# Newton steps and a scaling moved from VectorE and ScalarE to GpSimd, with a rewritten table of issue slots, in a fused attention and MLP kernel

## The chip, the core and the metric

One Trainium2 chip, one of its cores. The metric is the device time of one execution in microseconds (us), taken as the median of three runs. The five engines are TensorE (PE in the profile, with PEld for its weight loads), VectorE (DVE), ScalarE (ACT), GpSimd (POOL) and SyncE (SP, whose queue issues all DMAs here).

## What the program computes

```
def rmsnorm(x, g):
    rms = np.sqrt(np.mean(x * x, axis=-1, keepdims=True) + 1e-06)
    return x / rms * g
q_n, k_n = (rmsnorm(q, g_q), rmsnorm(k, g_k))
scores = (1.0 / np.sqrt(64)) * np.matmul(q_n, k_n.transpose(0, 1, 3, 2))
scores = scores - np.max(scores, axis=-1, keepdims=True)
attn = np.exp(scores)
attn = attn / (np.sum(attn, axis=-1, keepdims=True) + 1e-09)
attn_out = np.matmul(attn, v)                    # 8 batches, 12 heads, 448 tokens, 64 columns
x = attn_out.transpose(0, 2, 1, 3).reshape(3584, 768)
h = x @ w_in                                     # 768 x 2048
g = np.where(h > 0.0, h, np.exp(np.minimum(h, 0.0)) - 1.0)
out = g @ w_out                                  # 2048 x 768
```

All inputs and the output are float32.

## The kernel before

The matmuls run in float16. Each float32 operand is split into a high half and a low half (the rest after rounding), and a product is made of three matmuls: high by high, high by low, low by high.

The work is staged by batch. A batch has six pairs of heads (`p`, 48 in all) and each pair seven tiles of 128 queries (`T`, 336 in all). A tile passes: scores into one of five PSUM banks (`s_mm`, L547), row maximum on DVE (`s_max`, L559), exponential on ACT with its row sum (`s_exp`, L570), the sum plus 1e-9 on POOL (`s_z`, L577), the reciprocal on DVE (`s_rec`, L584), P's high half on ACT (`s_hi`, L609) and its low half on DVE (`s_lo`, L620), after which the bank is free for another tile. P is transposed by DMA (`s_tr`) or, for three pairs of the first batch, by PE with a diagonal that POOL makes (`s_diag`, `s_pe`). Seven tiles make an `attend(p)` on PE, whose output ACT and DVE evict (`x_high`, `x_low`).

Ahead of that, each pair's q and k are loaded, squared and summed; ACT makes a first inverse root from Ln and Exp (`qk_root`), and `qk_newton` (L384) sharpens it with one Newton step: four small DVE instructions on 128x14 numbers, at L387 (twice), L388 and L391. POOL multiplies by the result (`qk_norm`, L401).

The MLP of a batch starts when its six pairs are done. Each of its 16 hidden blocks ends in `m1_out` (L673): exp(h) on ACT (L682), `two`, (exp(h) - 1) times a scale on ACT (L686), a min and max against h on DVE (L690), then the high half on ACT (L695) and the low half on DVE (L698). The exponential's tile is called `e`.

While the first two batches run, the weights are converted too: `conv_in` for w_in's 16 blocks of 768 columns, `conv_out` for w_out's 24 of 512. Each takes two ACT instructions (L237, L238), two DVE instructions (L243, L267), a column sum on PE (L142), and steps on POOL (L291, or L322 and L331). Their working rooms are slices of three fixed tiles, `raws`, `wts` and `w32s`.

What sets the order of the work is a table, `SCHED`, written out by hand in half slots: two slots to a tile. A step listed at slot 14.5 is issued half a slot ahead of those at 15. Every engine executes its instructions in the order in which the slots issue them. A list `rate` says how many MLP matmuls have been issued by a given slot, so that they fill PE between the attention matmuls. From the third batch on one line of each kind is repeated.

Of the kernel before, what the change touches and what calls it, by code (L numbers as in the profile page):

```python
# [9 lines left out]
F16 = mybir.dt.float16  # L10
# [3 lines left out]
AF = mybir.ActivationFunctionType  # L14
ALU = mybir.AluOpType
# [8 lines left out]
NJ = 2 * S // 128  # L24
# [8 lines left out]
def tile_attention_then_elu_mlp(ctx: ExitStack, tc: tile.TileContext, qk, v, v_scan, gg, w_in, w_out, out):  # L33
# [184 lines left out]
    def conv(src, i, width, acol, bank, parts):  # L218
# [3 lines left out]
        raw = raw_in[i % len(raw_in)] if width == WI_W else room(raws, 2 * width, i)  # L222
        raw = raw.rearrange("p (n w) -> p n w", w=2)

        t, w = room(wts, width, i), room(w32s, width, i if width == WI_W else i + 2)
        ws = None

        def load():
# [154 lines left out]

    def qk_newton(p):  # L384
        ss, r0 = st1[p]
        for x, op0, op1 in ((D * 1e-6, ALU.add, ALU.mult), (-0.5 / D, ALU.mult, ALU.mult)):
            nc.vector.scalar_tensor_tensor(out=ss, in0=ss, scalar=x, in1=r0, op0=op0, op1=op1)  # L387
        nc.vector.scalar_tensor_tensor(  # L388
            out=r0, in0=ss, scalar=1.5, in1=r0, op0=ALU.add, op1=ALU.mult
        )  # L390
        nc.vector.tensor_scalar(  # L391
            out=r0[:, NJ:], in0=r0[:, NJ:], scalar1=kap, scalar2=None, op0=ALU.mult
        )
# [194 lines left out]

    def s_diag(T):
        dg = dgs[T] = pool.tile([128, 128], F32, tag="dgz", name="dgz", bufs=2)  # L590
        (nc.vector if DIAG_DVE else nc.gpsimd).tensor_scalar(
            out=dg, in0=ident, scalar1=stats[T][:, 2:3], scalar2=0.0, op0=ALU.mult, op1=ALU.add
        )

# [14 lines left out]
    def s_hi(T):  # L609
        if by_pe(T):  # L610
            ps, hi, _ = turned(T)
            nc.scalar.activation(hi, ps, AF.Copy)
            return
        if T < PB:
            p16 = p16s[T] = pfirst[(T - sum(p < T // NJ for p in PE_PAIRS) * NJ) % len(pfirst)]
        else:
            p16 = p16s[T] = pool.tile([128, 2 * S], F16, tag="p16", name="p16", bufs=3)
        nc.scalar.activation(p16[:, :S], pss[T][:, :S], AF.Copy, scale=stats[T][:, 2:3])  # L618
# [54 lines left out]
    def m1_out(b, f, ph):  # L673

        sc, isc, nisc, gsc = (t[:, f : f + 1] for t in mscale[b][:4])
        e = None
        g = gts[f]

        def one():
            nonlocal e  # L680
            e = pool.tile([128, S], F32, tag="e", name="e", bufs=3)
            nc.scalar.activation(e, ph[:, :S], AF.Exp, scale=sc)  # L682

        def two():

            nc.scalar.activation(e, e, AF.Identity, scale=isc, bias=nisc)  # L686

        def three():

            nc.vector.scalar_tensor_tensor(  # L690
                out=e, in0=e, scalar=0.0, in1=ph[:, :S], op0=ALU.min, op1=ALU.max
            )

        def four():
            nc.scalar.activation(g[:, 0], e, AF.Copy, scale=gsc)  # L695

        def five():
            nc.vector.scalar_tensor_tensor(  # L698
                out=g[:, 1], in0=e, scalar=gsc, in1=g[:, 0], op0=ALU.mult, op1=ALU.subtract
            )  # L700

        return [one, two, three, four, five]
# [84 lines left out]
    for T in reversed(range(NCHUNK)):  # L787
        k = 2 if by_pe(T) else 0 if T < PB else 1
        hs = [2 * T + h for h in SCHED["tile"][k]]
        j = T % NJ  # L790
        if k < 2:
            put(hs[:6], [(fn, T) for fn in (s_max, s_exp, s_z, s_rec, s_hi, s_lo)])


            at(hs[7 if j == 0 else 8 if j == NJ - 1 else 6], s_tr, T)
        else:
            put(hs, [(fn, T) for fn in (s_max, s_exp, s_z, s_rec, s_diag, s_pe, s_hi, s_lo)])
    for p in range(NP):
        k = p if p < 12 else 11
        put([h + HP * (p - k) for h in SCHED["qk"][k]], [  # L800
# [78 lines left out]
    for h in range(h + 1, h + 9):  # L879
# [3 lines left out]

SCHED = {
# [13 lines left out]
    ],  # L898
    "v": [
        [-2, 14, 15, 17, 18, 23, 24],  # L900
        [17, 23, 24, 24, 26, 36, 37],
        [26, 37, 38, 38, 40, 50, 51],
        [41, 52, 53, 54, 55, 65, 65],
        [54, 65, 66, 68, 68, 78, 79],
        [68, 79, 80, 82, 82, 93, 93],
        [82, 93, 94, 96, 96, 106, 106],
        [96, 107, 109, 109, 110, 120, 121],
        [110, 121, 122, 123, 124, 134, 135],
        [124, 135, 136, 137, 138, 147.5, 148.5],
        [138, 149, 150, 151, 152, 162, 162],  # L910
        [152.5, 163.5, 164.5, 165.5, 166.5, 176.5, 177.5],
    ],
    "scan": [
# [3 lines left out]
    ],  # L917
# [17 lines left out]
    ],  # L935
# [25 lines left out]
    ],  # L961
    "m": [
        [68, 69, 70, 72, 73, 74, 75, 77],
        [153, 154, 155, 156, 158, 159, 160.5, 161.5],
    ],
    "tile": [
# [3 lines left out]
    ],  # L970
    "rate": [
        [4, 8, 46, 104, 148, 188, 240, 288, 336, 382, 430, 478, 536, 576],
    ],
}
WO_OWN = 7

CK = S // 4
PE_PAIRS = (1, 3, 5)
DIAG_DVE = False

RATE_FROM = 85
UP = 13
# [38 lines left out]
```

## Time and profile before

| | us |
|---|---|
| median of 3 runs (lowest to highest) | 1270.25 (1269.4 to 1272.03) |
| the profiled execution, its own time | 1268.82 |
| its span | 1267.0 |
| PE busy | 1196.3 (94%) |
| DVE busy | 861.1 (68%) |
| ACT busy | 880.6 (70%) |
| POOL busy | 535.4 (42%) |

Busy time is the union of an engine's instructions in the trace. The difference between span and time is what lies around the program. Of the 40 equal slices of the span that the page shows, the first eight have a PE that is not fully busy; from the ninth slice on (from 260 us) it is busy throughout. The word head below means the first 260 us.

### The profile page before, as it was taken

To read this page: it belongs to the slowest core of one execution; us is meant where nothing else is said; L and a number is where in the kernel's file an instruction comes from. 1 tells how busy PE (TensorE), PEld (TensorE's weight loads), DVE (VectorE), ACT (ScalarE), POOL (GpSimd) and SP (SyncE) were. 2 spreads that over 40 slices of the span, in tenths; PEclk is the share of its full clock that TensorE was granted. 3 is DMA by queue.
4 is the path that set the end of the run, shared out by engine and by line. 5 is a ranking of instruction groups with operands and counts; after the bars stand their busy time and mean duration, and the time that the engine had idled before them with its cause. 6 is when DMAs were issued, how large, how long until landed. Compare 5 with 4: busy or idle time off the path is not lost.

```text
span 1267.0 us, 21793 instructions
## 1 busy us (share of the span) xinstructions
PE 1196.3 (94%) x7150; PEld 735.0 (58%) x7150; DVE 861.1 (68%) x1913; ACT 880.6 (70%) x1889; POOL 535.4 (42%) x858
## 2 busy tenths in 40 slices
PE   3778678999999999999999999999999999999998
PEld 2435444567556665576556755666557755676576
DVE  7888999986676567755785667756876677642310
ACT  6888789975797568855896578756886579643520
POOL 4766877664434343433434433334334333320000
PEclk9889799999999999999999999999999999999999
DMA  9967799999677986689577976798677968672012
GB/s 296 252 154 188 197 205 201 221 215 227 155 160 151 218 177 156 145 195 215 137 162 160 237 149 158 153 220 186 144 154 184 223 140 157 137 156 76 1 49 63
DMA packets 432979, 214.44 MB, mean 169 GB/s; under 512 B 389089, under 2 KB 409185, under 8 KB 432865
## 3 DMA queue, kind: packets, MB, share of 16 engines
q1 hardware_dynamic: 432864, 213.04, 74.1%
q8 instruction: 57, 0.93, 0.3%
q14 instruction: 58, 0.47, 0.1%
HBM read 93.52 MB, written 14.16 MB: 85 GB/s over the span
## 4 chain that ended last, share of the span: by engine, by line
PE 82%; DVE 10%; ACT 3%; POOL 3%; issue 1%; DMA 1%; SPq 0%; ACTq 0%; POOLq 0%
PE m L757 23%; PE m L743 20%; PE s L757 11%; PE s L743 10%; PE s L554 9%; PE av L658 7%; DVE w32s L267 2%; DVE st L561 1%; DVE wts L243 1%; DVE gall L698 1%; DVE p L628 1%; DVE ss L376 1%; DMA raws<-in_w_out 1%; PE s L599 1%; PE m L298 1%
## 5 line engine op out<-in xcount | busy, mean ns | idle before, releaser
L561 DVE TENSOR_REDUCE st<-s 128x1 f32<-128x448 f32 x336 | 208.3, 620 | 208.4 <-PE s L554 207.1
L579 POOL TENSOR_SCALAR st<-st 128x1 f32<-128x1 f32 x336 | 85.0, 253 | 496.7 <-ACT s L575 478.6
L743 PE MATMUL m<-x,whi 128*128 128x448 f16 x1020 | 281.9, 353 | 1.0 <-DVE x L669 1.0
L757 PE MATMUL m<-gall,whos 128*128 128x448 f16 x1024 | 282.2, 353 | 0.0
L757 PEld LDWEIGHTS <-whos 128*128 128x128 f16 x1536 | 221.5, 145 | 73.6 <-issue 1.1
L618 ACT ACTIVATE p<-s,st 128x448 f16<-128x448 f32 x294 | 185.9, 632 | 84.4 <-DMA pt<-p 51.1
L575 ACT ACTIVATE s<-s,st 128x448 f32<-128x448 f32 x315 | 190.5, 605 | 62.3 <-DVE st L561 62.1
L743 PEld LDWEIGHTS <-whi 128*128 128x128 f16 x1536 | 149.3, 98 | 136.1 <-issue 1.1
L628 DVE SCALAR_TENSOR_TENSOR p<-s,st,p 128x448 f16<-128x448 f32 x294 | 198.6, 676 | 14.0 <-ACT p L618 13.8
L554 PE MATMUL s<-qkt 128*128 128x448 f16 (+1 forms) x768 | 186.4, 363 | 19.6 <-DVE gall L625 11.2
L757 PE MATMUL m<-gall,wls 128*128 128x448 f16 x512 | 181.1, 354 | 0.0
L743 PE MATMUL m<-x,wli 128*128 128x448 f16 x510 | 179.8, 353 | 0.0
L743 PE MATMUL s<-x,whi 128*128 128x448 f16 x516 | 141.7, 352 | 0.0
L757 PE MATMUL s<-gall,whos 128*128 128x448 f16 x512 | 141.2, 353 | 0.0
L757 PEld LDWEIGHTS <-wls 128*128 128x128 f16 x768 | 110.6, 144 | 41.4 <-issue 6.5
L743 PEld LDWEIGHTS <-wli 128*128 128x128 f16 x768 | 75.1, 98 | 76.1 <-issue 8.4
L698 DVE SCALAR_TENSOR_TENSOR gall<-e,gsc,gall 128x448 f16<-128x448 f32 x128 | 98.5, 769 | 24.1 <-ACT gall L695 24.1
L554 PEld LDWEIGHTS <-qkt 128*128 128x128 f16 (+1 forms) x768 | 62.6, 101 | 86.0 <-issue 45.1
L658 PE MATMUL av<-pt,vt 128*64 128x448 f16 x990 | 102.0, 354 | 1.0 <-DVE most L145 1.0
L695 ACT ACTIVATE gall<-e,gsc 128x448 f16<-128x448 f32 x128 | 85.2, 666 | 18.1 <-DVE e L690 17.7
L686 ACT ACTIVATE e<-e,nisc,isc 128x448 f32<-128x448 f32 x128 | 97.1, 758 | 0.3
L665 ACT ACTIVATE x<-av 128x448 f16<-128x448 f32 x48 | 26.0, 542 | 96.1 <-PE av L658 70.1
(120 smaller groups left out, 1778.7 us busy)
## 6 DMA issues: line engine op xcount, KB each, us to landing
wls<-wl_d SPq DMA_DIRECT2D x48, 512.0 KB, 4.2
nat<-in_qk SPq DMA_DIRECT2D x48, 448.0 KB, 3.6
raws<-in_w_out SPq DMA_DIRECT2D x24, 512.0 KB, 4.9
qkt<-qkt SPq DMA_DIRECT2D x96, 112.0 KB, 2.3
out<-y SPq DMA_DIRECT2D x48, 224.0 KB, 2.8
vn<-in_v SPq DMA_DIRECT2D x38, 256.0 KB, 3.4
vscan<-in_v_scan SPq DMA_DIRECT2D x36, 224.0 KB, 4.0
whos<-in_w_in SPq DMA_DIRECT2D x10, 768.0 KB, 6.7
```

Of the source, the lines that this page charges most:

```text
L554: nc.tensor.matmul(ps[r0 : r0 + n, :S], lhs, qq[:, 1, h * S : h * S + S], start=(t == 0), stop=(t == 2),)
L561: nc.vector.tensor_reduce(out=st[:, 0:1], in_=pss[T][:, :S], axis=AX.X, op=ALU.max, negate=True)
L575: nc.scalar.activation(e, ps, AF.Exp, bias=st[:, 0:1], accum_out=st[:, 1:2])
L579: nc.gpsimd.tensor_scalar(out=st[:, 1:2], in0=st[:, 1:2], scalar1=1e-9, scalar2=2.0 ** (UP - 7) if by_pe(T) else 2.0**-7, op0=ALU.add, op1 ...
L618: nc.scalar.activation(p16[:, :S], pss[T][:, :S], AF.Copy, scale=stats[T][:, 2:3])
L628: nc.vector.scalar_tensor_tensor(out=p16[:, S:], in0=ps[:, :S], scalar=r, in1=p16[:, :S], op0=ALU.mult, op1=ALU.subtract)
L658: nc.tensor.matmul(av[64 * h : 64 * h + 64, :S], vs[:, h], ps[h], start=(k == 0), stop=(k == len(terms) - 1),)
L686: nc.scalar.activation(e, e, AF.Identity, scale=isc, bias=nisc)
L695: nc.scalar.activation(g[:, 0], e, AF.Copy, scale=gsc)
L698: nc.vector.scalar_tensor_tensor(out=g[:, 1], in0=e, scalar=gsc, in1=g[:, 0], op0=ALU.mult, op1=ALU.subtract)
L743: nc.tensor.matmul(ph[:, :S], w[:, c, :], x[:, r, :], start=(c == 0 and i == 0), stop=last)
L757: nc.tensor.matmul(py[:, :S], w, g[:, r, :], start=(f == 0 and i == 0), stop=last)
```

## The change

`qk_newton` runs on POOL for the pairs 2 to 11, as six instructions where DVE has four, since DVE's fused form is split into a tensor-scalar and a tensor-tensor instruction. `two` runs on POOL for the first batch's MLP (16 instructions). P's halves of every fourth tile of the second batch (T = 43, 47 to 83) lie in the third 512-column room of `wts`, where the other tiles go round three buffers; w_out's conversion goes round the first two rooms of `wts` in place of three. A flag that was off (`DIAG_DVE`) is taken out. The table `SCHED` has new numbers in most rows of the first two batches.

```diff
-        t, w = room(wts, width, i), room(w32s, width, i if width == WI_W else i + 2)
+        t = room(wts if width == WI_W else wts[:, : 2 * WO_W], width, i)
+        w = room(w32s, width, i if width == WI_W else i + 2)
...
     def qk_newton(p):
         ss, r0 = st1[p]
+        if p in NEWTON_POOL:
+            ts, tt = nc.gpsimd.tensor_scalar, nc.gpsimd.tensor_tensor
+            ts(out=ss, in0=ss, scalar1=D * 1e-6, scalar2=-0.5 / D, op0=ALU.add, op1=ALU.mult)
+            tt(out=ss, in0=ss, in1=r0, op=ALU.mult)
+            tt(out=ss, in0=ss, in1=r0, op=ALU.mult)
+            ts(out=ss, in0=ss, scalar1=1.5, scalar2=1.0, op0=ALU.add, op1=ALU.mult)
+            tt(out=r0, in0=ss, in1=r0, op=ALU.mult)
+            ts(
+                out=r0[:, NJ:], in0=r0[:, NJ:], scalar1=kap, scalar2=0.0, op0=ALU.mult,
+                op1=ALU.add,
+            )
+            return
...
+        elif T < 2 * PB and T % 4 == 3:
+
+            p16 = p16s[T] = wts[:, 2 * WO_W : 2 * WO_W + S].bitcast(F16)
         else:
             p16 = p16s[T] = pool.tile([128, 2 * S], F16, tag="p16", name="p16", bufs=3)
...
-            nc.scalar.activation(e, e, AF.Identity, scale=isc, bias=nisc)
+            if b in TWO_POOL:
+                nc.gpsimd.tensor_scalar(
+                    out=e, in0=e, scalar1=-1.0, scalar2=isc, op0=ALU.add, op1=ALU.mult
+                )
+            else:
+                nc.scalar.activation(e, e, AF.Identity, scale=isc, bias=nisc)
...
-        [26, 37, 38, 38, 40, 50, 51],
+        [26, 37, 38, 38, 41, 52, 52],
...
-        [4, 8, 46, 104, 148, 188, 240, 288, 336, 382, 430, 478, 536, 576],
+        [2, 4, 46, 98, 142, 186, 238, 288, 334, 388, 428, 478, 536, 576],
...
+NEWTON_POOL = range(2, 12)
+TWO_POOL = (0,)
```

In that row of `v`, the last two numbers are the slots of `x_high` and `x_low` for the pair 2; the row of `rate` says that by slot 106 the changed kernel has issued 98 MLP matmuls instead of 104, and by slot 134 the same 288. In `wi` the slot of the low half's first eviction (L302) stands one slot later in the first seven of 16 rows, and in `v` the slot of `x_high` one or two slots later for the pairs 0, 1, 2 and 4.

Three places in the order of the instructions follow. Line numbers in rows of the changed kernel are its own: L600, L644, L574 there are L587, L628, L561 before.

DVE in the first batch, around slot 7, before: the Newton step of the pair 2 stands between the low half of P (`x_133`) and a scan of v.

```order
L151 TENSOR_SCALAR ws<-a_in 128x1
L587 RECIPROCAL st<-st 128x1
L628 SCALAR_TENSOR_TENSOR x_133<-s_68,st,x_133 128x448
L387 SCALAR_TENSOR_TENSOR ss<-ss,r_330 128x14 x2
L388 SCALAR_TENSOR_TENSOR r_330<-ss,r_330 128x14
L391 TENSOR_SCALAR r_330<-r_330,kap 128x7
L180 TENSOR_REDUCE mv<-gall 128x1
L267 SCALAR_TENSOR_TENSOR w32s<-whos,wts 128x768
```

The same place on DVE in the changed kernel:

```order
L151 TENSOR_SCALAR ws<-a_in 128x1
L180 TENSOR_REDUCE mv<-gall 128x1
L600 RECIPROCAL st<-st 128x1
L644 SCALAR_TENSOR_TENSOR x_133<-s_68,st,x_133 128x448
L180 TENSOR_REDUCE mv<-gall 128x1
L268 SCALAR_TENSOR_TENSOR w32s<-whos,wts 128x768
```

The four instructions are gone from DVE's queue, and one scan of v has moved ahead of the reciprocal.

POOL in the first batch, around slot 19, before, where the tiles of the pair 1 need a row sum (`st`) and a diagonal (`dgz`) each:

```order
L579 TENSOR_SCALAR st<-st 128x1
L471 COPY vt<-vt 64x384 x2
L424 TENSOR_TENSOR t_470<-nat,t_470 128x7x64
L591 TENSOR_SCALAR dgz<-ident,st 128x128
L579 TENSOR_SCALAR st<-st 128x1
L591 TENSOR_SCALAR dgz<-ident,st 128x128
L401 TENSOR_TENSOR nat<-nat,r_518 128x896
```

The same place on POOL in the changed kernel (`ss` and `r_544` are the pair 3's sums and roots):

```order
L592 TENSOR_SCALAR st<-st 128x1
L484 COPY vt<-vt 64x384 x2
L389 TENSOR_SCALAR ss<-ss 128x14
L390 TENSOR_TENSOR ss<-ss,r_544 128x14
L391 TENSOR_TENSOR ss<-ss,r_544 128x14
L392 TENSOR_SCALAR ss<-ss 128x14
L393 TENSOR_TENSOR r_544<-ss,r_544 128x14
L394 TENSOR_SCALAR r_544<-r_544,kap 128x7
L604 TENSOR_SCALAR dgz<-ident,st 128x128
L592 TENSOR_SCALAR st<-st 128x1
L604 TENSOR_SCALAR dgz<-ident,st 128x128
L414 TENSOR_TENSOR nat<-nat,r_544 128x896
```

Six instructions stand ahead of a diagonal and a row sum, and the 128x448 subtraction L424 (L437 in the changed kernel) that stood there has moved ahead of this place.

ACT in the second batch, at the first hidden block, before (`p_1916` and the like are P's buffers, `e` the exponential):

```order
L618 ACTIVATE p_1916<-s_67,st 128x448
L682 ACTIVATE e<-m_74,sc 128x448
L575 ACTIVATE s_70,st<-s_70,st 128x448
L327 ACTIVATE whos<-w32s 128x512
L686 ACTIVATE e<-e,nisc,isc 128x448
L618 ACTIVATE p_1958<-s_68,st 128x448
L372 ACTIVATE qkt<-nat 128x896
```

ACT at this place in the changed kernel, and then POOL where the first two `e` stand:

```order
L634 ACTIVATE p_1938<-s_67,st 128x448
L588 ACTIVATE s_70,st<-s_70,st 128x448
L328 ACTIVATE whos<-w32s 128x512
L698 ACTIVATE e<-m_74,sc 128x448
L423 ACTIVATE t_1967<-nat 128x7x64
L634 ACTIVATE p_1977<-s_68,st 128x448
L373 ACTIVATE qkt<-nat 128x896
```

```order
L592 TENSOR_SCALAR st<-st 128x1
L703 TENSOR_SCALAR e<-e,isc 128x448
L323 TENSOR_SCALAR w32s<-w32s,ws 128x512
L332 TENSOR_TENSOR w32s<-w32s,whos 128x512
L592 TENSOR_SCALAR st<-st 128x1
L444 TENSOR_TENSOR t_1967<-nat,t_1967 128x7x64
L703 TENSOR_SCALAR e<-e,isc 128x448
```

The instruction L686 is gone from ACT; on POOL it stands behind a row sum and ahead of two steps of a weight's conversion.

## Rows read from the trace of the kernel before

**Rows 1.** Windows, five stretches: PE, PEld, DVE, ACT, POOL busy; PE clock; DMA share.

```profile
0.00:20.00 20.00, 4.12 (x31) 2.89 (x32) 13.45 (x35) 10.81 (x18) 5.29 (x10) 1.00 0.91 282
20.00:100.00 80.00, 58.09 (x394) 33.72 (x394) 71.29 (x148) 68.06 (x151) 55.40 (x76) 0.85 0.89 221
100.00:170.00 70.00, 51.78 (x392) 34.16 (x391) 66.37 (x147) 57.17 (x129) 53.86 (x72) 0.85 0.76 192
170.00:260.00 90.00, 78.91 (x544) 43.68 (x542) 86.87 (x177) 83.42 (x172) 65.16 (x79) 1.00 1.00 209
260.00:1140.00 880.00, 880.00 (x5134) 540.86 (x5134) 600.39 (x1374) 622.76 (x1363) 353.58 (x615) 1.00 0.78 174
```

**Rows 2.** Waits of PE, whole span: waited for, us in total, times, longest.

```profile
PE s L142 <- DVE wts L243: 15.9, 2, 13.7
PE s L554 <- DVE gall L625: 11.2, 11, 2.3
```

**Rows 3.** The page, chain that ended last, shares of the span by engine.

```profile
PE 82%; DVE 10%; ACT 3%; POOL 3%; issue 1%; DMA 1%; SPq 0%; ACTq 0%; POOLq 0%
```

**Rows 4.** Instruction groups by form, DVE, 20 to 260 us: count, busy us, mean ns.

```profile
L387 DVE SCALAR_TENSOR_TENSOR ss<-ss,r 128x14 f32<-128x14 f32 x20 | 6.1, 307 | 0.3
L391 DVE TENSOR_SCALAR r<-r,kap 128x7 f32<-128x7 f32 x10 | 3.8, 375 | 0.4
L388 DVE SCALAR_TENSOR_TENSOR r<-ss,r 128x14 f32<-128x14 f32 x10 | 1.7, 174 | 0.3
...
L267 DVE SCALAR_TENSOR_TENSOR w32s<-raws,wts 128x512 uint32<-128x512 uint32 x22 | 21.9, 997 | 0.1
L243 DVE SCALAR_TENSOR_TENSOR wts<-wts,w32s 128x512 uint32<-128x512 uint32 x22 | 19.1, 869 | 1.2 <-ACT w32s L238 1.2
L243 DVE SCALAR_TENSOR_TENSOR wts<-wts,w32s 128x768 uint32<-128x768 uint32 x14 | 17.7, 1262 | 1.4 <-ACT w32s L238 1.4
L698 DVE SCALAR_TENSOR_TENSOR gall<-e,gsc,gall 128x448 f16<-128x448 f32 x15 | 16.0, 1064 | 0.0
L267 DVE SCALAR_TENSOR_TENSOR w32s<-whos,wts 128x768 uint32<-128x768 uint32 x10 | 13.3, 1328 | 0.1
```

**Rows 5.** Chain, windows 30 to 33 and 221 to 223 us: shares by line.

```profile
by line: DVE mv L180 39.4%; DVE x L628 19.4%; DVE st L561 17.7%; DVE ss L387 9.2%; DVE r L391 7.7%; DVE r L388 6.2%; DVE ws L151 5.1%; DVE a_in L145 4.7%; issue 3.1%; DVE st L587 2.4%
...
by line: DVE ss L387 52.8%; DVE p L628 29.8%; DVE st L561 26.0%; DVE r L388 9.2%; issue 8.5%; DVE st L587 7.8%; DVE r L391 2.0%
```

**Rows 6.** Single lines of source, whole span: count, least, median and greatest ns.

```profile
L243 DVE SCALAR_TENSOR_TENSOR wts<-wts,w32s x40: 666/949/1708, 12.7 to 270.7; 128x512 uint32<-128x512 uint32 x24, 128x768 uint32<-128x768 uint32 x16
...
L267 DVE SCALAR_TENSOR_TENSOR w32s<-whos,wts x10: 939/1268/1859, 21.7 to 120.8; 128x768 uint32<-128x768 uint32 x10
...
L698 DVE SCALAR_TENSOR_TENSOR gall<-e,gsc,gall x128: 661/676/2133, 179.0 to 1211.8; 128x448 f16<-128x448 f32 x128
```

**Rows 7.** Timeline around 249 us: start us, duration us, instruction.

```profile
248.66 1.69 POOL L401 TENSOR_TENSOR nat<-nat,r 128x896 f32<-128x896 f32 x1
248.69 2.13 DVE L698 SCALAR_TENSOR_TENSOR gall<-e,gsc,gall 128x448 f16<-128x448 f32 x1
```

**Rows 8.** POOL: line L579 to 270 us (ns); group L322, 20 to 260 us.

```profile
L579 POOL TENSOR_SCALAR st<-st x72: 189/192/776, 24.9 to 267.7; 128x1 f32<-128x1 f32 x72
...
L322 POOL TENSOR_SCALAR w32s<-w32s,ws 128x512 f32<-128x512 f32 x20 | 15.5, 778 | 1.6 <-DVE ws L151 0.7
```

**Rows 9.** Instruction groups, ACT, 170 to 260 us.

```profile
L686 ACT ACTIVATE e<-e,nisc,isc 128x448 f32<-128x448 f32 x16 | 12.2, 763 | 0.0
```

**Rows 10.** Waits of ACT, then of DVE, 20 to 260 us.

```profile
ACT x L665 <- PE av L658: 6.7, 4, 3.3
ACT wli L302 <- PE m L299: 3.4, 5, 1.2
...
DVE x L669 <- ACT x L665: 2.7, 3, 1.9
```

**Rows 11.** Windows, one stretch, columns as in rows 1.

```profile
140.00:160.00 20.00, 16.32 (x116) 11.62 (x116) 19.09 (x43) 14.97 (x35) 18.82 (x26) 0.77 0.75 203
```

More of the change, by code (lines that the diff above doesn't have):

```diff
@@ L590, in s_diag @@
         dg = dgs[T] = pool.tile([128, 128], F32, tag="dgz", name="dgz", bufs=2)
-        (nc.vector if DIAG_DVE else nc.gpsimd).tensor_scalar(
+        nc.gpsimd.tensor_scalar(
             out=dg, in0=ident, scalar1=stats[T][:, 2:3], scalar2=0.0, op0=ALU.mult, op1=ALU.add
@@ L684, in two @@
         def two():
-            nc.scalar.activation(e, e, AF.Identity, scale=isc, bias=nisc)
+            if b in TWO_POOL:
+                nc.gpsimd.tensor_scalar(
+                    out=e, in0=e, scalar1=-1.0, scalar2=isc, op0=ALU.add, op1=ALU.mult
+                )
+            else:
+                nc.scalar.activation(e, e, AF.Identity, scale=isc, bias=nisc)
         def three():
@@ L796, in tile_attention_then_elu_mlp @@
         else:
-            put(hs, [(fn, T) for fn in (s_max, s_exp, s_z, s_rec, s_diag, s_pe, s_hi, s_lo)])
+            put(hs, [
+                (fn, T)
+                for fn in (s_max, s_exp, s_z, s_rec, s_diag, s_pe, s_hi, s_lo)
+            ])
     for p in range(NP):
@@ L899 @@
     "v": [
-        [-2, 14, 15, 17, 18, 23, 24],
-        [17, 23, 24, 24, 26, 36, 37],
-        [26, 37, 38, 38, 40, 50, 51],
-        [41, 52, 53, 54, 55, 65, 65],
-        [54, 65, 66, 68, 68, 78, 79],
+        [-2, 14, 15, 17, 18, 24, 26],
+        [17, 23, 24, 24, 26, 37, 37],
+        [26, 37, 38, 38, 41, 52, 52],
+        [41, 52, 53, 54, 55, 65, 65.5],
+        [54, 65, 66, 68, 70, 80, 80.5],
         [68, 79, 80, 82, 82, 93, 93],
-        [82, 93, 94, 96, 96, 106, 106],
+        [81.5, 92.5, 93.5, 95.5, 95.5, 105.5, 106],
         [96, 107, 109, 109, 110, 120, 121],
@@ L909 @@
         [124, 135, 136, 137, 138, 147.5, 148.5],
-        [138, 149, 150, 151, 152, 162, 162],
+        [138.5, 149.5, 150.5, 151, 152, 162, 162],
         [152.5, 163.5, 164.5, 165.5, 166.5, 176.5, 177.5],
@@ L959 @@
         [136.5, 140.5, 141.5, 143.5, 145.5, 147.5, 147.5, 148.5, 150.5, 152.5],
[1 row of a table removed]
[1 row of a table added]
     ],
     "m": [
-        [68, 69, 70, 72, 73, 74, 75, 77],
+        [68, 69, 72, 72, 73, 75, 75, 77],
         [153, 154, 155, 156, 158, 159, 160.5, 161.5],
@@ L978 @@
 PE_PAIRS = (1, 3, 5)
-DIAG_DVE = False
+NEWTON_POOL = range(2, 12)
+TWO_POOL = (0,)
 RATE_FROM = 85
```

73 rows, old and new, of the table SCHED are left out of this document.

## The prediction

> **What bounds the kernel now.** I read the windows first, since the answer differs by stage. After 260 us PE has no idle time: 880.00 of 880 us [rows 1]. Nothing that the change does there can shorten the run, and what it does there is little, since the Newton steps of the pairs 12 to 47 and the scaling of the batches 1 to 7 stay where they were. All idle time of PE lies in the head: 20 - 4.12 = 15.9 us in the first stretch, then 21.9, 18.2 and 11.1, in sum 67.1 us [rows 1]. The MLP matmuls that have been issued by slot 134 and by slot 176 are the same in both tables (288 and 576), so the time changes by what these 67.1 us change, and by the clock.
>
> The waits of PE, read next, name DVE: it waits for converted weights (L243) and for P's low half (L625), which frees a bank [rows 2]. The 13.7 us of the longest one are the start, before any weight is converted, and stay. DVE is busy 71.29 + 66.37 + 86.87 = 224.5 of 240 us from 20 to 260 us, ACT 208.7, POOL 174.4 [rows 1]. A busy share does not tell who is waited for, so the third view is the chain that ended last: DVE has 10%, ACT and POOL 3% each of the span's 1267 us, thus 127, 38 and 38 us [rows 3]. As PE alone leads from 260 us on, these shares belong to the head: DVE leads in 127/260 = 49% of it, ACT and POOL in 15% each. I use these as weights: a microsecond taken from an engine's queue somewhere in the head shortens the head by its weight. That is a choice; the bounds below are 0 and 1.
>
> **The Newton steps leave DVE.** Ten pairs, four instructions each: 20 x 307 ns at L387, 10 x 174 at L388 and 10 x 375 at L391 are 6.1 + 1.7 + 3.8 = 11.6 us of DVE [rows 4]. Not all of them lay on the path. From 30 to 33 us the chain ran over one burst: 9.2 + 7.7 + 6.2% of 3 us are 0.69 us; from 221 to 223 us over another, 64% of 2 us, 1.28 us [rows 5]. These two alone, 2.0 us, are the lower end, all 11.6 us the upper; by DVE's weight it is -5.7 us, which lies between.
>
> **POOL takes 26 us more.** No row shows a tensor-scalar or tensor-tensor of 128x14 on POOL. The nearest is L579 with one column: 189 ns at the least, 192 in the median, 776 at the most [rows 8]. Six of them are 1.1 us a burst at the least; at twice that they would be 2.3 us. I take 0.25 us each, somewhat above the nearest row since 14 columns and two inputs cost something: 1.5 us a burst, 15 us for ten (bounds 11 and 23). The scaling of `e` reads 448 columns in one input; L322 does this with 512 in 778 ns [rows 8], so 0.68 us, times 16 is 10.9 us (0.6 to 0.9 each). Sum 26 us, and POOL is busy 200 of 240 us. Queued behind each burst is a row sum or a diagonal (second order fence of the change), and behind these the reciprocal on DVE, P's halves, the bank and at last the scores' matmul. By POOL's weight: 26 x 0.15 = +3.9 us (0 if bursts fall where POOL waits for ACT anyway, 26 if each reaches PE).
>
> **DVE pays for a busier POOL.** DVE's instructions with both inputs in SBUF are longer in the head than they need to be: L243 and L267 on 512 columns take 869 and 997 ns where the least is 666, on 768 columns 1262 and 1328 where the least is 939, L698 takes 1064 where the median of the run is 676 [rows 4, 6]. The excess is 22 x 0.203 + 22 x 0.331 + 14 x 0.323 + 10 x 0.389 + 15 x 0.388 = 26 us. The timeline shows why: POOL's L401 started at 248.66 for 1.69 us, DVE's L698 at 248.69, and it took 2.13 us: POOL's end and some 0.5 us behind it [rows 7]. Against 174 us of POOL time that is 0.15 us of DVE for each us of POOL; 26 us more make 3.9 us, by DVE's weight +1.9 us (0 to 9.6, the third rival's figure).
>
> **The scaling of `e` leaves ACT.** 16 x 763 ns are 12.2 us [rows 9], in a stretch in which ACT is busy 83.4 of 90 us, but DVE 86.9 [rows 1]; DVE stays in the way there. By ACT's weight -1.8 us (0 to -12.2).
>
> **The moved slots.** Four evictions of `attend` (L665) let ACT wait 6.7 us for PE, five of a weight's low half (L302) 3.4 us, and DVE waited 2.7 us behind the first [rows 10]. These are the steps that the table moves later. If all these waits went they would be worth 10.1 x 0.15 + 2.7 x 0.49 = 2.8 us; a later eviction holds its bank longer, so I take -2.0 (+2 to -2.8). I found no price for the other moves of half a slot: 0, with 3 us either way. The new `rate` only shifts six matmuls within the part of the head that ends at slot 134: 0.
>
> **The places for P and `wts`.** w_out's conversion has two rooms instead of three. ACT writes a room again at the earliest two slots after PE's sum and DVE's join of it are issued, so it waits only where those run late; P's fourth place takes away waits of P's writer for the transposing DMA, which after 260 us cost nothing. I cost both at 0 (-1 to +3).
>
> **The clock.** From 20 to 170 us the granted clock is 0.85, after that 1.00 [rows 1]; in these 150 us PE is busy only 109.9. At 0.85 some 30% of the 150 us are at 1.2 GHz. With a tenth of the idle time gone a tenth of the loss may go with it: of PE's 109.9 us some 33 ran at 1.2 GHz, half of that, 16 us, is the bound. A tenth of it is 1.6 us, and not all of it is on the path: -1.0 (+3 to -6).
>
> **Sum.** -5.7 + 3.9 + 1.9 - 1.8 - 2.0 - 1.0 = -4.7 us. The profiled execution took 1268.82 us, so its like would take 1264.1; the median before is 1270.25, and against it I predict 1265.5 us. A difference of 0.2%, 2.5 us, is about what a measurement of this kernel can tell from no change.
>
> **Rivals.**
>
> First: DVE leads everywhere in the head, and all of its relief counts. For it: 94% busy from 20 to 260 us, and the longest waits of PE name it. Against: ACT and POOL hold 76 us of the chain. Then -11.6 + 3.9 + 1.9 - 1.8 - 2.8 and -3.0 for the clock are -13.4: 1256.9 us.
>
> Second, slower: POOL becomes what PE waits for. Its queue is in order, and a burst or an `e` that stands ahead of a tile's row sum delays that tile's low half on DVE, hence its bank. For it: between 140 and 160 us POOL is busy 18.82 of 20 us [rows 11], with no room for a burst, and PE is busy only 16.32. Against: elsewhere POOL is idle a quarter of the time, and the table moves POOL's long steps away from the bursts. It decides once more than a third of the 26 us arrives at PE: 26 x 0.33 = 8.6 = 5.7 + 1.8 + 2.0 + 1.0 - 1.9. With half of them it is 13 - 8.6 = +4.4: 1274.7 us.
>
> Third, no difference: the work has changed its engine, but DVE stands still for it. Each us of POOL that falls beside one of DVE's two-input instructions blocks it for that us. These are busy 21.9 + 19.1 + 17.7 + 16.0 + 13.3 = 88 of 240 us, 37% [rows 4], so 26 us more on POOL take 9.6 from DVE, 4.7 by its weight instead of 1.9, and the sum is -1.9: 1268.4 us. For it are the 2.13 us of L698. Against it: many POOL instructions are too short to meet one, and the same 37% of the present 174 us would be 64 us of excess, where 26 are seen.
>
> The Trainium skill states this rule (SBUF — State Buffer, "Who interferes with whom"): a DVE instruction with two SBUF inputs and a GpSimd instruction that reads SBUF exclude each other, and whichever comes first holds the shared ports for its whole length; and it warns (Perfetto Trace Analysis, "Optimizing Scalar/DVE Operations") that moving work between these two "might not help". The trace agrees with the exclusion: 2.13 us where the median is 676 ns [rows 6, 7].
>
> **How the numbers follow.** Chances: the forecast's case 0.48 (own range 1261 to 1267.5), the first rival 0.18, the second 0.17, the third 0.17. Faster by over 0.2%: 0.48 + 0.18 = 0.66; within 0.2%: 0.17; slower: 0.17. The range is to hold 8 in 10: from 1256.5, at which half of the first rival's spread is left out, to 1273, at which some two thirds of the second is.
>
> **What would show it.** On the path: PE's waits in the head should sum to about 62 us, those for L625 and L628 fewer, and PE should be full from about 255 us. On DVE no burst between 20 and 250 us, and its busy time there some 8 us less. POOL's busy time up by 26 us, a burst 1.5 us long. L243, L267 and L698 should be a little longer than before; if their excess grows from 26 to over 32 us, the third rival holds. DVE waiting for L579 by over 8 us in sum, or PE waiting for the diagonals of POOL, would be the second. Wrong throughout would be a PE that idles after 260 us: ACT or DVE would then be late in the second batch's MLP.

## The result, and the profile after

The changed kernel takes 1276.7 us (four runs, 1275.09 to 1278.0) against 1270.0 of the kernel before: a ratio of 1.0045 with an interval of 1.003 to 1.006 (the two medians alone give 1.0053). All differences in time between runs below are taken from such ratios. Forecast were 1265.5 us, in a range from 1256.5 to 1273, so the sign was wrong and the range too low. It is the side of the second rival (1274.7 us).

Windows of the changed kernel, the same stretches and columns as [rows 1]:

```profile
0.00:20.00 20.00, 4.27 (x31) 2.94 (x32) 13.59 (x35) 10.46 (x17) 5.43 (x10) 1.00 0.91 282
20.00:100.00 80.00, 58.20 (x412) 34.51 (x412) 68.47 (x133) 69.26 (x156) 62.94 (x101) 0.89 0.90 223
100.00:170.00 70.00, 49.24 (x357) 32.70 (x355) 60.29 (x130) 54.52 (x121) 58.98 (x88) 0.81 0.75 186
170.00:260.00 90.00, 78.98 (x526) 41.56 (x523) 79.81 (x154) 71.50 (x152) 76.67 (x106) 0.98 0.84 195
260.00:1140.00 880.00, 878.38 (x5133) 539.47 (x5132) 603.21 (x1380) 622.94 (x1362) 359.39 (x618) 1.00 0.78 174
```

PE now idles 69.3 us in the head (67.1 before) and 1.6 us after it. The rest of the 7.6 us between the two spans is busy time: 1200.0 us of PE in place of 1196.3, for the same matmuls, with a granted clock of 0.89, 0.81 and 0.98 in the second to fourth stretch where it was 0.85, 0.85 and 1.00: higher once and lower twice. POOL is busy 24 us more from 20 to 260 us, DVE 16 us less and ACT 13 us less, and both are late all the same. The waits tell why. First three lines of the kernel before that the prediction did not need (engine and line, what it waited for: us in total, times, longest; PE over the span, ACT and DVE from 20 to 260 us):

```profile
PE s L599 <- POOL dgz L591: 2.9, 3, 2.5
...
ACT whos L327 <- POOL w32s L322: 1.5, 3, 0.8
...
DVE st L587 <- POOL st L579: 3.3, 4, 1.1
```

The same three in the changed kernel, with those that answer to [rows 2] and [rows 10]:

```profile
PE s L142 <- DVE wts L244: 15.7, 2, 13.5
...
PE s L567 <- DVE gall L641: 9.2, 7, 2.2
PE s L612 <- POOL dgz L604: 9.1, 8, 3.8
...
ACT whos L328 <- POOL w32s L323: 16.5, 11, 2.9
...
ACT x L681 <- PE av L674: 3.1, 3, 1.7
...
ACT wli L303 <- PE m L300: 1.1, 3, 0.5
...
DVE st L600 <- POOL st L592: 13.3, 14, 2.9
```

All three engines that POOL serves wait for it: PE for a diagonal 6.2 us longer, ACT for the first step of w_out's conversion 15 us longer, DVE for the row sum 10 us longer. The waits that the table was to shorten did get shorter (L681: 3.1 of 6.7; L303: 1.1 of 3.4). In the chain that ended last, the page's line by engine answers to [rows 3]: POOL goes from 3% to 6% of the span, DVE from 10% to 7%.

```profile
PE 80%; DVE 7%; POOL 6%; ACT 3%; issue 2%; DMA 1%; SPq 0%; POOLq 0%; ACTq 0%
```

The place around slot 19, which the second pair of order fences ahead of the prediction shows, in the timeline of the changed kernel (start us, duration us, instruction, in brackets the idle time before it and what ended it): POOL's part, then DVE's and PE's.

```profile
50.23 1.04 POOL L484 COPY vt<-vt 64x384 f16<-64x384 f16 x2
51.36 0.80 POOL L389 TENSOR_SCALAR ss<-ss 128x14 f32<-128x14 f32 x1
...
53.45 0.29 POOL L394 TENSOR_SCALAR r<-r,kap 128x7 f32<-128x7 f32 x1
53.73 0.37 POOL L604 TENSOR_SCALAR dgz<-ident,st 128x128 f32<-128x128 f32 x1
54.18 0.19 POOL L592 TENSOR_SCALAR st<-st 128x1 f32<-128x1 f32 x1
...
51.12 0.96 DVE L268 SCALAR_TENSOR_TENSOR w32s<-raws,wts 128x768 uint32<-128x768 uint32 x1
54.40 0.16 DVE L600 RECIPROCAL st<-st 128x1 f32<-128x1 f32 x1 [2.32 <-POOL st L592]
...
54.15 2.05 PE L612 MATMUL s<-dgz,ex 128*112 128x128 f32 x8 [3.85 <-POOL dgz L604]
```

The burst, the six instructions of one pair's Newton step, runs from 51.36 to 53.74 us. The row sum behind it takes 0.19 us, but DVE, whose queue is in order too, stands still for 2.32 us until it is there, and PE for 3.85 us until the diagonal is.

The new work on POOL, groups by form from 20 to 260 us (count, busy us, mean ns, idle time before):

```profile
L703 POOL TENSOR_SCALAR e<-e,isc 128x448 f32<-128x448 f32 x15 | 14.0, 932 | 2.1 <-ACT e L698 1.6
...
L394 POOL TENSOR_SCALAR r<-r,kap 128x7 f32<-128x7 f32 x10 | 4.2, 415 | 1.0
...
L393 POOL TENSOR_TENSOR r<-ss,r 128x14 f32<-128x14 f32 x10 | 3.6, 364 | 0.8
...
L389 POOL TENSOR_SCALAR ss<-ss 128x14 f32<-128x14 f32 x10 | 3.1, 305 | 0.8
L392 POOL TENSOR_SCALAR ss<-ss 128x14 f32<-128x14 f32 x10 | 2.5, 246 | 0.9
...
L391 POOL TENSOR_TENSOR ss<-ss,r 128x14 f32<-128x14 f32 x10 | 2.2, 218 | 0.8
L390 POOL TENSOR_TENSOR ss<-ss,r 128x14 f32<-128x14 f32 x10 | 2.2, 217 | 0.8
```

The bursts cost 17.8 us (15 were taken), the scaling 16 x 0.932 = 14.9 us (10.9 were taken): 32.7 us instead of 26. At the least time of each of these lines in this trace it would have been 10 x 1.36 + 16 x 0.627 = 23.6 us, so some 9 us came on top where they ran. And DVE's two-input instructions, which answer to [rows 4]:

```profile
L244 DVE SCALAR_TENSOR_TENSOR wts<-wts,w32s 128x512 uint32<-128x512 uint32 x21 | 19.6, 931 | 0.4 <-ACT w32s L239 0.4
L244 DVE SCALAR_TENSOR_TENSOR wts<-wts,w32s 128x768 uint32<-128x768 uint32 x14 | 18.2, 1302 | 0.0
L268 DVE SCALAR_TENSOR_TENSOR w32s<-raws,wts 128x512 uint32<-128x512 uint32 x20 | 17.4, 868 | 0.1
L719 DVE SCALAR_TENSOR_TENSOR gall<-e,gsc,gall 128x448 f16<-128x448 f32 x14 | 15.5, 1107 | 4.3 <-ACT gall L716 4.3
L268 DVE SCALAR_TENSOR_TENSOR w32s<-whos,wts 128x768 uint32<-128x768 uint32 x10 | 12.7, 1270 | 0.1
```

By the same least times as in the prediction their excess is 21 x 0.265 + 14 x 0.363 + 20 x 0.202 + 14 x 0.431 + 10 x 0.331 = 24 us, not more than the 26 of before.

### The profile page after: what moved, and what is told of

Same layout as the page of the kernel before. It is cut to its first block, busy times and chain, and to the rows that moved or that the text cites. A ratio compares the mean times of both kernels' runs of the same rounds, so it can differ in the third digit from the quotient of the medians.

```text
span 1274.6 us, 21843 instructions
## 1 busy us (share of the span) xinstructions
PE 1200.0 (94%) x7150; PEld 736.4 (58%) x7150; DVE 851.3 (67%) x1873; ACT 871.4 (68%) x1873; POOL 568.9 (45%) x934
## 4 chain that ended last, share of the span: by engine, by line
PE 80%; DVE 7%; POOL 6%; ACT 3%; issue 2%; DMA 1%; SPq 0%; POOLq 0%; ACTq 0%
PE m L778 23%; PE m L764 20%; PE s L778 11%; PE s L764 10%; PE s L567 8%; PE av L674 7%; DVE wts L244 1%; DVE w32s L268 1%; POOL w32s L332 1%; DVE st L574 1%; POOL st L592 1%; PE s L612 1%; POOL nat L414 1%; DVE ss L377 1%; ACT s L588 1%
## 5 line engine op out<-in xcount | busy, mean ns | idle before, releaser
L574 DVE TENSOR_REDUCE st<-s 128x1 f32<-128x448 f32 x336 | 208.7, 621 | 212.8 <-PE s L567 211.4
L634 ACT ACTIVATE p<-s,st 128x448 f16<-128x448 f32 x283 | 179.1, 633 | 77.6 <-DMA pt<-p 33.5
L644 DVE SCALAR_TENSOR_TENSOR p<-s,st,p 128x448 f16<-128x448 f32 x283 | 191.6, 677 | 13.9 <-ACT p L634 13.1
L719 DVE SCALAR_TENSOR_TENSOR gall<-e,gsc,gall 128x448 f16<-128x448 f32 x128 | 100.1, 782 | 28.7 <-ACT gall L716 28.7
L681 ACT ACTIVATE x<-av 128x448 f16<-128x448 f32 x48 | 26.1, 545 | 95.2 <-PE av L674 66.1
L764 PE MATMUL s<-x,wli 128*128 128x448 f16 x258 | 91.3, 354 | 0.0
```

The lines of the kernel that those rows point to most:

```text
L574: nc.vector.tensor_reduce(out=st[:, 0:1], in_=pss[T][:, :S], axis=AX.X, op=ALU.max, negate=True)
L644: nc.vector.scalar_tensor_tensor(out=p16[:, S:], in0=ps[:, :S], scalar=r, in1=p16[:, :S], op0=ALU.mult, op1=ALU.subtract)
L681: nc.scalar.activation(xs[p % NX][:, 0], av[:, :S], AF.Copy)
L719: nc.vector.scalar_tensor_tensor(out=g[:, 1], in0=e, scalar=gsc, in1=g[:, 0], op0=ALU.mult, op1=ALU.subtract)
L764: nc.tensor.matmul(ph[:, :S], w[:, c, :], x[:, r, :], start=(c == 0 and i == 0), stop=last)
```

## The experiments

Each was timed beside the kernel before on the same chip. "Against before" is (ratio - 1) x 1270 us; an interval of the ratio reaches 1.1 to 1.8 us to either side. A difference between two rows is clear of noise from about 2 us on.

| run | edit | median us | ratio (interval) | against before |
|---|---|---|---|---|
| e1 | changed, Newton back on DVE | 1270.8 | 0.9996 (0.9987 to 1.0005) | -0.5 |
| e2 | changed, scaling of `e` back on ACT | 1273.7 | 1.0020 (1.0011 to 1.0029) | +2.5 |
| e3 | changed, both back: table and places | 1267.1 | 0.9975 (0.9966 to 0.9984) | -3.2 |
| e4 | changed, old table | 1279.5 | 1.0073 (1.0060 to 1.0086) | +9.3 |
| r5 | changed, row sums on DVE | 1267.6 | 0.9972 (0.9963 to 0.9982) | -3.6 |
| r6 | e3, row sums on DVE | 1265.5 | 0.9958 (0.9945 to 0.9971) | -5.3 |
| r7 | table only | 1267.2 | 0.9973 (0.9963 to 0.9982) | -3.4 |
| r8 | e3, Newton of four pairs on POOL | 1266.8 | 0.9966 (0.9956 to 0.9977) | -4.3 |
| c1 | before, new rows `v` and `wi` only | 1266.1 | 0.9962 (0.9949 to 0.9974) | -4.8 |
| c2 | r6, Newton on POOL | **1261.7** | 0.9928 (0.9916 to 0.9941) | -9.1 |
| c3 | r6, Newton of four pairs on POOL | 1265.1 | 0.9953 (0.9941 to 0.9966) | -6.0 |
| c4 | e3, row sums of pairs 1, 3, 5 on DVE | 1266.8 | 0.9966 (0.9952 to 0.9979) | -4.3 |
| d1 | r5, `e` on POOL 16 columns wide | 1264.4 | 0.9944 (0.9933 to 0.9955) | -7.1 |
| d2 | c2 without the new places, a spare POOL instruction per `e` | 1267.2 | 0.9972 (0.9960 to 0.9984) | -3.6 |
| d3 | c1, row sums on DVE, Newton on POOL | 1267.5 | 0.9976 (0.9966 to 0.9986) | -3.0 |

**Each part undone.**

```diff
-NEWTON_POOL = range(2, 12)      # e1, e3
+NEWTON_POOL = ()
-TWO_POOL = (0,)                 # e2, e3
+TWO_POOL = ()
```

In e4, `SCHED` is that of the kernel before and the rest as changed.

> The changed kernel with the ten Newton steps back on VectorE, all else as changed. Theory A, POOL's queue is what PE, DVE and ACT now wait for: POOL's busy time from 20 to 260 us falls by some 18 us (ten bursts of 1.78), DVE's wait for the row sum (13.3 us) falls below 9, PE's wait for POOL's diagonals (9.1 us) below 6, and the time falls by 2 to 5 us, to 1272 to 1275. Theory B, the new table's slots are what costs: the bursts only fill gaps of POOL, and with 11.6 us more on DVE the time stays or rises, 1276 to 1281.

> The changed kernel with the scaling of e back on ScalarE, all else as changed. Theory A: POOL loses 15 us between 170 and 260 us, ACT's wait for POOL's first step of w_out (16.5 us) falls below 6, the tiles of slots 112 to 130 no longer fall behind, and the time falls by 2 to 4 us, to 1273 to 1275. Theory B: ACT has 12 us more to do there, and the time stays within 1 us of 1276.7 or rises.

> The changed kernel with both moves undone: the new table and the new places for P alone. Theory A: all POOL waits are as in the kernel before, PE waits for POOL's diagonals some 3 us, and the time is that of the kernel before or less, 1266 to 1271. Theory B: the table or the places cost the time by themselves, 1275 or more. In between (1271 to 1275) both have a share, read from the difference to the kernel before.

> The changed kernel with the table of the kernel before: both moves and the places alone. Theory A: POOL has the same 32 us more, in slots that were not made for it, so that PE waits for diagonals at least as long as in the changed kernel (9 us or more), 1276 to 1283. Theory B: without the new slots the time is near the kernel before or under it, 1264 to 1271.

All four times came out as theory A has it, e1 with more than it expected. Other expected numbers did not: in e2 ACT's wait for w_out's step stayed at 10.3 us (below 6 expected), in e4 PE's wait for diagonals was 8.2 us (9 or more), and POOL's busy time fell by 12 us in e1 (18 expected) and by 9 us from 170 to 260 us in e2 (15). Against e3, Newton alone costs 5.7 us (e2), the scaling alone 2.7 (e1), both 8.9 (the changed kernel; 9.6 by medians, the figure in the expectation of r6), so the two prices nearly add up. On the old table, both with the places make +9.3, and with the moves in place the new table is thus worth 9.3 - 5.7 = 3.6 us. So the table is the gain and the moves are the loss. The chains of e3 and then e2 show the swap when Newton alone goes to POOL: DVE gives up 5% of the span, and POOL takes them.

```profile
PE 81%; DVE 11%; ACT 3%; POOL 2%; issue 2%; DMA 1%; SPq 0%; ACTq 0%; DVEq 0%; POOLq 0%
```

```profile
PE 80%; POOL 7%; DVE 6%; ACT 3%; issue 2%; DMA 1%; SPq 0%; POOLq 0%; ACTq 0%
```

The waits of DVE and ACT in e1, then in e2, tell the two moves apart: the wait for the row sum comes from Newton, the wait for w_out's step from both (it is 2.3 us in e3).

```profile
DVE st L600 <- POOL st L592: 2.9, 2, 1.9
...
ACT whos L328 <- POOL w32s L323: 7.8, 6, 3.1
```

```profile
DVE st L600 <- POOL st L592: 13.1, 13, 2.9
...
ACT whos L328 <- POOL w32s L323: 10.3, 9, 1.8
```

**The row sum off POOL's queue.** r5 and r6 take from the path what the burst is said to delay, not the burst.

```diff
-        nc.gpsimd.tensor_scalar(
+        (nc.vector if T < 70 else nc.gpsimd).tensor_scalar(
             out=st[:, 1:2], in0=st[:, 1:2], scalar1=1e-9,
```

> The changed kernel with the row sum's step (sum plus 1e-9, 128x1) of the tiles below 70 on VectorE instead of GpSimd. Theory A, the row sum that stands behind the bursts in POOL's queue is what the path waits for: POOL loses some 67 x 0.32 = 21 us in the head, DVE gains 67 x 0.15 = 10, DVE's wait for the row sum (13.3 us) is gone, and the time falls to 1267 to 1273 although DVE has more to do. Theory C, the row sum's place does not matter, DVE's own work does: 10 us more on DVE and the time rises, 1279 to 1283.

> The same step on VectorE where Newton and the scaling of e are back on their old engines (the control for the run before; without it that kernel took 1267.1). Theory A: POOL's queue was not in the way there, so only DVE's 10 us count, 1270 to 1275; the two moves then cost under 3 us instead of 9.6. Theory C: the difference between the two stays near 9.6.

The two moves now cost 1.7 us, inside the noise, where they cost 8.9. DVE has 70 instructions more (142 ns in the median, 9.9 us) in both r5 and r6, and yet r5 is faster than the changed kernel by 9.3 us and r6 than e3 by 2.2. The expectation of r6 (slower than e3) was wrong, and POOL's busy time from 20 to 260 us fell by 10 us in r5 where 21 were expected. That the trip ACT to POOL to DVE was on the path even without the moves is argued from these 2.2 us, which are barely clear of noise; POOL also has 70 instructions less.

> New table and places, row sums below tile 70 on VectorE, all ten Newton steps on GpSimd, the scaling of e on ScalarE. Against the control with both moves undone (1265.5) and the one with both (1267.6). Theory A: off the row sum's queue a burst costs nothing and DVE's 11.6 us count a little, 1263 to 1266; the remaining 2 us are then those of e. If Newton still costs 0.65 us each: 1271 or more.

> As the run before with only the four Newton steps that stand in gaps of POOL (pairs 2, 4, 5, 6) on GpSimd. Theory A: 1263.5 to 1265.5, the lowest of all so far or level with it, since both single edits gave 0.3 and 1.6 us. If the two gains are the same one: 1265.5 to 1266.5.

Newton on POOL turns from +5.7 us to -3.8 (c2 against r6), more than expected. c2 is the fastest of all, 0.9928 (0.9916 to 0.9941) of the kernel before. DVE's wait for POOL's row sum, 13.1 us in e2, is gone, ACT's for w_out's step is 2.8 us (10.3 in e2), and c2 is 11.7 us faster than e2. A rival is that POOL simply has less to do in c2. It can't be all: e2 and d2 (below) have POOL busy equally long, and d2, whose row sums are on DVE, is 6.1 us faster although DVE is busy longer. The stretch from 20 to 260 us in e2, then in d2:

```profile
20.00:260.00 240.00, 189.83 (x1324) 112.10 (x1323) 210.83 (x426) 208.31 (x451) 191.43 (x283) 0.91 0.87 207
...
20.00:260.00 240.00, 192.57 (x1339) 112.81 (x1338) 218.75 (x509) 212.84 (x460) 192.10 (x235) 0.91 0.88 210
```

The burst at slot 19 is still there, as long as in the changed kernel, but DVE doesn't wait for it; the timeline of c2, DVE and then POOL:

```profile
50.17 0.14 DVE L592 TENSOR_SCALAR st<-st 128x1 f32<-128x1 f32 x1
50.23 0.95 DVE L268 SCALAR_TENSOR_TENSOR w32s<-raws,wts 128x768 uint32<-128x768 uint32 x1
51.09 0.16 DVE L600 RECIPROCAL st<-st 128x1 f32<-128x1 f32 x1
...
50.42 0.82 POOL L389 TENSOR_SCALAR ss<-ss 128x14 f32<-128x14 f32 x1
...
52.82 0.72 POOL L604 TENSOR_SCALAR dgz<-ident,st 128x128 f32<-128x128 f32 x2
```

The reciprocal comes at 51.09 us, where the changed kernel had it at 54.40 (0.9 us of that is a head start: L268 begins at 50.23 against 51.12). PE waits for diagonals in c2 nearly as long as in the changed kernel (8.2 us and 9.1), so that wait, though the prediction named it, was not what decided.

```profile
PE s L612 <- POOL dgz L604: 8.2, 5, 3.6
```

**Where a burst finds a gap.** r8 moves only the Newton steps of the pairs 2, 4, 5 and 6 (row sums on POOL, as in the kernel before).

> New table and places, the scaling of e on ScalarE, and only the Newton steps of the pairs 2, 4, 5 and 6 on GpSimd, which fall at about 31, 72, 97 and 121 us, where POOL is busy under 70 percent of the time. Theory A: there a burst finds a gap, DVE is relieved of 4.6 us, and the time is 1264 to 1268 against 1267.1 with none moved and 1273.7 with ten moved. If a burst costs the same wherever it stands (0.65 us each by the ten): 1269 to 1270.5.

Its four bursts cost nothing (-1.1 us, inside the noise), and DVE waits little for the row sum, where ten bursts made it 13.1 us:

```profile
DVE st L600 <- POOL st L592: 3.6, 3, 1.9
```

By difference the other six cost 5.7 + 1.1 = 6.8 us, 1.1 each. So bursts do not all cost the same. That the place in the queue decides, and not how many bursts there are, is argued: the six alone were not run.

With the row sums on DVE it is the other way: c3 with four bursts gains 3.1 us less than c2 with ten; its time is within what was expected, but it isn't the lowest.

**The table.**

> The new table alone: both moves undone, and P's places and the rooms of w_out's conversion as before. If the table makes the gain of 3.4 us that the kernel with table and places shows, 1266 to 1268.5; if the places make it, 1269.5 to 1272.

> The kernel before with the new rows of `v` and `wi` alone (the later evictions of attend and of a weight's low half among them), no move and no new places. If these evictions make the table's gain of 3.5 us, as the prediction had it (-2.0): 1266.5 to 1269. If the gain lies in the other rows: 1269.5 to 1272.

The places are worth nothing (r7 against e3). The later evictions, with the other new numbers in `v` and `wi`, give all of the table's gain (-4.8 us; the 1.4 more than r7 are inside the noise). The evictions were not run without those other numbers. The waits of ACT that [rows 10] shows as 6.7 and 3.4 us are down to 1.6 and 0.2 in c1:

```profile
ACT x L681 <- PE av L674: 1.6, 2, 1.0
...
ACT wli L303 <- PE m L300: 0.2, 1, 0.2
```

> The table of before with the new rows of `v` and `wi`, row sums below tile 70 on VectorE, the ten Newton steps on GpSimd, the scaling of e on ScalarE, P's places as before. If the other new rows of the table are worth nothing, as the 1266.1 against 1267.2 says: 1260 to 1262.5. If they make room for the Newton steps: 1263 to 1266.

Without the other new rows of the table, c2's gain is not there (-3.0 against -9.1, more lost than either case expected): row sums and Newton together, which took 5.9 us off e3, take nothing off c1. So these rows, or c2's places for P, which d3 lacks, make room for the Newton steps. Which of them do was not tried, and c1 with the row sums alone was not run.

**The price of `e`.** r5 is 5.6 us slower than c2, though no row sum stands in POOL's queue and ACT has 12 us less to do. d1 narrows POOL's part to `e[:, :16]`, which leaves the other columns unscaled. d2 leaves the scaling on ACT and gives POOL an instruction of that size on a room that nobody reads. For that room it gives up P's new places, and DVE fills it once:

```diff
+            if b == 0:
+                w = wts[:, 2 * WO_W : 2 * WO_W + S]
+                if f == 0:
+                    nc.vector.memset(w, 1.0)
+                nc.gpsimd.tensor_scalar(
+                    out=w, in0=w, scalar1=0.0, scalar2=isc, op0=ALU.mult, op1=ALU.add
+                )
```

> Row sums below tile 70 on VectorE, both moves as changed, but the scaling of e on GpSimd covers 16 of its 448 columns (the other 432 stay unscaled). Theory T, POOL's time on e is the price (ScalarE waits for GpSimd's first step of w_out behind it, VectorE shares its port): POOL loses some 10 us, and the time falls from 1267.6 to 1260 to 1263. Theory H, the trip through GpSimd's queue is the price: 1265.5 to 1268.

> Row sums below tile 70 on VectorE, Newton on GpSimd, the scaling of e on ScalarE, P's places as before; beside each of the 16 scalings GpSimd runs an instruction of the same shape on a room that nobody reads. Theory T: the time rises from 1261.7 to 1265 to 1269. Theory H: 1261 to 1263.

d2 is theory T's: POOL's time alone, with no trip, costs 5.5 us, if the places are worth as little here as in r7. d1 lies between the two theories, 3.6 us faster than r5. The line's row in d1, and then in r5 (count, least, median and greatest ns), offers a reason: the narrow instruction still takes 588 ns in the median, so 6.5 us were taken away and not 10.

```profile
L703 POOL TENSOR_SCALAR e<-e,isc x16: 272/588/992, 171.1 to 245.8; 128x16 f32<-128x16 f32 x16
```

```profile
L703 POOL TENSOR_SCALAR e<-e,isc x16: 634/996/1267, 173.2 to 250.5; 128x448 f32<-128x448 f32 x16
```

What POOL's time does there is seen in the stretch from 170 to 260 us, windows and waits, of r5 and then of c2:

```profile
170.00:260.00 90.00, 82.81 (x551) 45.70 (x548) 86.36 (x190) 75.01 (x159) 74.06 (x88) 0.98 0.92 210
...
ACT whos L328 <- POOL w32s L323: 9.2, 8, 2.3
...
L719 DVE SCALAR_TENSOR_TENSOR gall<-e,gsc,gall 128x448 f16<-128x448 f32 x16 | 18.5, 1155 | 1.8 <-ACT gall L716 1.7
```

```profile
170.00:260.00 90.00, 85.80 (x589) 48.84 (x586) 86.58 (x202) 88.74 (x185) 65.05 (x75) 1.00 0.96 216
...
L719 DVE SCALAR_TENSOR_TENSOR gall<-e,gsc,gall 128x448 f16<-128x448 f32 x16 | 15.3, 958 | 0.0
```

ACT is busy 13.7 us less in r5, of which some 12 are the 16 scalings; it waits 9.2 us for POOL's L323, which stands behind `e`, a wait that c2 has not in this stretch. L719 takes 3.2 us longer on DVE. How the 5.6 us divide between these two was not separated. In d2 the price is about the same, but there the instruction that is L719 in c2 takes 957 ns in the mean (958 in c2), while ACT waits 4.3 us for L323: this price came without a longer L719.

**Row sums of some tiles.**

> New table and places, both moves undone, and the row sum on VectorE only for the 21 tiles whose sum feeds a diagonal (pairs 1, 3 and 5). If the gain of 1.6 us of the control comes from these tiles, whose diagonal waits for two trips between the engines: 1264.5 to 1266. If it comes from the other 49: 1266.5 to 1267.5.

Its 1266.8 us is in the range of the second case, but with 0.9966 it lies between e3 (0.9975) and r6 (0.9958), inside the intervals of both: inconclusive.

## Why the prediction was wrong

- **What bounds the kernel** was right: all of the difference arises in the head, but for 1.6 us behind it (behind 260 us a matmul takes 173 ns of PE on average in both kernels), and DVE is what PE waits for most, before and after.
- **"By POOL's weight: 26 x 0.15 = +3.9 us"** is the step that failed. The four terms of the moves were to make -5.7 + 3.9 + 1.9 - 1.8 = -1.7 us, and the moves cost 8.9. A quarter more came on POOL (32.7 us), but what failed is the weight. Even with no relief of DVE and ACT at all, 8.9 of 32.7 us would be 0.27 of each microsecond, not 0.15. With the reliefs as measured for DVE in c2 against r6 (-3.8) and as forecast for ACT (-1.8), POOL is left with 8.9 + 3.8 + 1.8 = 14.5 us, 0.44 of each microsecond: an estimate, since that relief was measured with the row sums on DVE. In the place of a share the runs showed a wait: DVE stood still 13.3 us for the row sum behind the bursts, where it had been 3.3, and Newton's loss went with that wait in e1 and in c2. The weight came from the chain of the kernel before. That tells how much of POOL's present work was waited for; it says nothing of work put ahead of a row sum that every tile waits for. The prediction had read off the order that "queued behind each burst is a row sum or a diagonal" and still priced it as an average.
- **The second rival** was the right mechanism, with 13 us for POOL where the estimate is 14.5; and its sign was named: DVE's wait for the row sum over 8 us (13.3). It got a chance of 0.17 since POOL seemed idle a quarter of the time elsewhere. r8 shows what that idle time is worth: four bursts fit into it, the other six, by difference, did not.
- **Newton leaving DVE, -5.7 us:** the nearest measurement, c2 against r6, is -3.8, and it holds what the bursts on POOL still cost. The term was of the right size there, with the row sums on DVE and the whole new table; without these (e2, d3) it was not to be had.
- **DVE lengthened by POOL, +1.9, and the third rival:** the excess stayed at 24 us, so both are refuted in sum. (The prediction used L243's least of 666 ns for L267 too, whose own least is 674 ns; that is 0.2 of its 26 us.) The Trainium skill's rule that DVE and GpSimd exclude each other at the shared ports (SBUF — State Buffer, "Who interferes with whom") shows in single rows [rows 7], and no run makes it the price of Newton. The Trainium skill's warning that the move "might not help" (Perfetto Trace Analysis, "Optimizing Scalar/DVE Operations") held, for a reason of queue order.
- **The scaling of `e`, -1.8:** ACT did get 12 us less to do, but with both moves its wait for POOL's step of w_out went from 1.5 to 16.5 us (7.8 with this one alone, e1), and this move alone costs 2.7 us (e1 against e3).
- **The moved slots, -2.0 (+2 to -2.8):** right in sign, and the waits named did get shorter, but mis-sized: -4.8 us with `v` and `wi` alone, -3.4 with the whole table, both past the bound of -2.8, the second within the noise. Either the weights (2.8 for all these waits) were too small here as well, or the other new numbers in `v` and `wi` helped; no run shows which. The new `rate` moves six matmuls once more at slot 148, which the prediction overlooked; it was not run apart.
- **Places, 0:** right. **The clock, -1.0:** not borne out; the matmuls took 3.7 us longer, at a granted clock of 0.90 from 20 to 260 us where it was 0.91. This rests on one profiled execution each. How much of the 3.7 us is the clock's, and whether PE's waits lowered it, is not shown.

By the runs, then, the table gives -3.4 us, the places +0.2, and the moves +8.9, as the difference of the changed kernel to e3; what the clock adds within them was not measured apart.

## What to carry to other kernels

Price work that is moved to a less busy engine by what stands behind it in that engine's queue, one place at a time: ask how long the next short instruction that another in-order engine waits for is held up. A share of the chain is a price for work that is already there, not for work put in front of a link of it. Before moving work onto an engine, take off that engine the tiny steps that every tile passes through: 0.14 us on the busiest engine was cheaper than a trip through the queue of a less busy one, and it turned the same move from +5.7 us to -3.8. It did so with a table of slots rewritten around the move; with most of the old table (d3) the gain was not there.

## What the runs showed that was not expected

On POOL the width says little for small tiles: at the least, 128x1 takes 189 ns [rows 8], 128x14 212 (L389), but 128x7 287 (L394) and 128x16 272 (L703 in d1), where 128x448 takes 627. Among the other instructions the means are well above the least: 932 for these 627 ns in the changed kernel. The granted clock from 100 to 170 us differs between single executions with the same table, with no move made in either (they differ in P's places, worth nothing): 0.78 in e3's profile (1269.1 us) and 0.88 in r7's (1266.6 us). So a clock term of 1 us can't be read from one profile of each kernel.
